# Attention ahead of two expert layers: row sums copied and then inverted in halves, block-diagonal keys from the load, late conversions ordered behind the last exponential, results over four buffers

## The chip, the cores and the metric

One core of a Trainium2 chip runs the whole program. The metric is the device time of one launch in microseconds. Lower is better. TensorE does matmuls and transposes, VectorE and ScalarE do elementwise work (both read and write PSUM and SBUF), SyncE (SP) issues the transfers, GpSimd only sets a few constants at the start.

## What is computed

Four batches of 12 heads, 448 positions, head size 64:

```python
scores = scale * np.matmul(q, k.transpose(0, 1, 3, 2))
scores = cap * np.tanh(scores / cap)
attn = np.exp(scores - max)            # divided by the row's sum
attn_out = np.matmul(attn, v)
x = attn_out as [1792 tokens, 768]
h = x @ w_in;   g = h - np.tanh(h);                     x = g @ w_out     # 768 -> 2048 -> 768
h = x @ w_in2;  g = h / (1.0 + np.exp(-1.702 * h));     out = g @ w_out2
```

The expert weights arrive as 64-bit floats; the kernel turns them into 32-bit numbers itself. All is float32 outside.

## The kernel before, in words

**Pairs.** Attention works on pairs of heads; there are 24 pairs, `g` from 0 to 23, six to a batch. For a pair, `load_qk` (L229) issues two q and four k transfers on SP and `load_v` (L248) three. The 448 keys are three chunks of 128 and a rest of 64. The rest of both heads is put into one block-diagonal 128 x 128 tile, so that one matmul serves both heads. `prep_q` (L261) transposes q on TensorE (four times 112 columns) and VectorE copies it out of PSUM. `prep_k` (L270) transposes three 128 x 128 pieces and, at L277, the rest with 64 rows and 64 columns; VectorE copies the three chunks (L79) and then the two 64 x 64 blocks of the rest into the tile `kt`, whose other blocks were set to zero once. `scores` (L284) writes the score matrix with keys on the partitions, for the rest (chunk KC) and chunks 0, 1, 2. `pair_act` (L298) takes tanh and exponential on ScalarE. `key_adds` (L311) adds the exponentials of the chunks on VectorE (`ts`), `pair_sum` (L331) sums them over keys on TensorE into one PSUM tile of a batch (`ps_r`, a single buffer), `pair_pv` (L319) multiplies by v and `pair_out` (L340) copies the result (`xs`).

**Row sums.** When a batch's six pairs are done, `batch_recip` (L347) inverts the sums in one VectorE instruction straight out of PSUM and sends them to `wrow` in device memory. `w_rows` (L353) broadcasts a pair's rows back from there, and the pair's x is multiplied by it (L370), rounded by ScalarE (`xh`) and its rest taken by VectorE (`xl`, L82). Batches 0 and 1 do so during attention at the pairs in `split_at` (L363); batches 2 and 3 put x unscaled into device memory (`xd`), and `x_next` (L585) does the rest within the last layer of the first pass.

**Weights.** There are chunks of weights, 128 x 768 or 128 x 640 numbers each. Conversion of a chunk has six steps: `conv_exp` (L158, ScalarE), `conv_low` (L162, VectorE or ScalarE), `conv_shift` and `conv_or` (L171, L175, VectorE), `conv_hi` (L182, ScalarE) and `conv_lo` (L186, VectorE), which also sends both halves to device memory (`kept`) for the second pass. Nine chunks, `early`, are converted during attention at the pairs in `conv_at` (L362). `prepare` (L193) loads or converts the next chunks in order, two ahead of the one in use (`LEAD`).

**The two layers' matmuls.** The tokens are worked in two passes of two batches. A pass has `gemm_in(0)` (L505), `gemm_out` (L524), `gemm_in(1)` and `gemm_out_rows` (L546). Every product is three matmuls of rounded parts. `gemm_out_rows` works the 384 result columns of a half in seven blocks of 128 tokens over eight steps `j`; in step 7 each block is finished, and `rows_out` (L570) copies it, on ScalarE for even and VectorE for odd blocks, into a two-buffer tile (tag "q") and sends it out in two transfers. `ps_next` (L453) gives eight PSUM banks in turn. In steps 0 to 7 of the first half and 0 to 3 of the second half of the first pass one `x_next` is put on the list `late`, which runs within the following step.

**What sets the order.** In attention each compute instruction goes through `pin`, so each engine keeps the order of the program. A planner places everything else, the transfers and all behind attention among them, where it finds the operands and the engine free; it may place it between the pinned instructions. The loop over pairs of `attention` (L365) is the hand-written order: the activations of the rest and chunk 0, scores of chunks 1 and 2, their activations, `pair_sum` of the pair before, PV of chunk 0, early conversions, `batch_recip`, transposes for pair g+2, PV of the rest, first scores of pair g+1, `key_adds`, PV of chunks 1 and 2. In the last pair 12 matmuls of the first layer, and 5 more behind it, stand between the last ones of attention.

Of the kernel before, what the change touches and what calls it, by code (L numbers as in the profile page):

```python
# [37 lines left out]
def attention_moe_moe(ctx, tc, q, k, v, cap, w_in1, w_out1, w_in2, w_out2, out):  # L38
# [79 lines left out]
    kt = [one_p.tile([P, P], F32, name=f"kt{i}") for i in range(3)]  # L118
# [110 lines left out]
    def load_qk(g):  # L229
        if g >= NG:  # L230
            return
        b, hp = divmod(g, NP)
        t = raw_p.tile([P, 2, 2 * C * D], F32, tag="raw", name="raw")
        for j in range(2):
            a = slice(j * D, (j + 1) * D)
            nc.sync.dma_start(
                out=t[:CP, 0].rearrange("p (c e) -> p c e", c=C)[:, :, a],
                in_=q[b, 2 * hp + j].rearrange("(p c) d -> p c d", c=C),
            )
        for j in range(2):  # L240
            a = slice(j * D, (j + 1) * D)
            kk = t[:, 1].rearrange("p (c e) -> p c e", c=C)
# [17 lines left out]

    def prep_q(g):  # L261
        if g >= NG:
            return
        qkt[g] = st_p.tile([P, 2, S], F32, tag="qk", name="qk")
# [3 lines left out]
        hi_dve(qkt[g][:, 0], ps[:, :S])  # L268

    def prep_k(g):  # L270
        if g >= NG:
            return
        ps = ps_s.tile([P, 512], F32, tag="s", name="ps_qk")
        t = raw.pop(g)
        for c in range(KC):
            pin(nc.tensor.transpose(ps[:, c * P:(c + 1) * P], t[:, 1, c * P:(c + 1) * P], ident))
        pin(nc.tensor.transpose(ps[:, KC * P:S], t[:KT, 1, KC * P:(KC + 1) * P], ident[:KT, :KT]))  # L277
        cp = hi_act if g == 0 else hi_dve
        cp(qkt[g][:, 1, :KC * P], ps[:, :KC * P])
        for j in range(2):  # L280
            a = slice(j * D, (j + 1) * D)
            cp(kt[g % 3][a, a], ps[a, KC * P:S])

    def scores(g, c):  # L284
        if g >= NG:
            return
        ps = ps_b.tile([P, 2, 512], F32, tag="b", name="ps_sc")
        if c == KC:
            pin(nc.tensor.matmul(ps[:, 0, :S], kt[g % 3], qkt[g][:, 0], start=True, stop=True))  # L289
        else:  # L290
            for j in range(2):
                a = slice(j * D, (j + 1) * D)
                pin(nc.tensor.matmul(  # L293
                    ps[:, j, :S], qkt[g][a, 1, c * P:(c + 1) * P], qkt[g][a, 0], start=True, stop=True
                ))
        sc_t[g, c] = ps

    def pair_act(g, cs):  # L298
# [9 lines left out]
        for c in cs:  # L308
            pin(nc.scalar.activation(out=tt[g, c], in_=tt[g, c], func=AF.Exp, scale=cpos))
# [52 lines left out]
    conv_at = [(2, 3), (4, 5), (7, 8), (9, 10), (11, 13), (14, 15), (16, 17), (19, 20), (21, 22)]  # L362
    split_at = [8, 9, 10, 11, 13, 14, 15, 16, 17, 19, 20, 21]  # L363

    def attention():  # L365
        wb = {}

        def scaled_x(g):
            x = xs[g]
            pin(nc.vector.tensor_tensor(out=x, in0=x, in1=wb.pop(g), op=ALU.mult))  # L370

        load_qk(0)
        load_v(0)
        load_qk(1)
# [4 lines left out]
        load_v(1)  # L379
        load_qk(2)  # L380
        prep_q(1)
        prep_k(1)
        for g in range(NG):
            x_g = split_at.index(g) if g in split_at else None
            pair_act(g, (KC, 0))
            for n, (p1, p2) in enumerate(conv_at):
                if g == p2 + 1:
                    conv_hi(early[n])
# [6 lines left out]
            for n, (p1, p2) in enumerate(conv_at):  # L395
                if g == p1 - 1:
                    conv_exp(early[n])
            load_v(g + 2)
            if g > 0:
                pair_sum(g - 1)  # L400
            pair_pv(g, 0)
            for n, (p1, p2) in enumerate(conv_at):
                if g == p1:
                    conv_low(early[n])
                elif g == p2:
                    conv_shift(early[n])
# [10 lines left out]
            if g + 1 in split_at:  # L417
                n = split_at.index(g + 1)
# [5 lines left out]
            if g == NG - 2:  # L424
                prepare(1)
            if g == NG - 1:
# [3 lines left out]
                hold[0] = False  # L430
# [6 lines left out]
        hold[0] = True  # L437
# [4 lines left out]
        batch_recip(B - 1)  # L442
# [156 lines left out]
    nc.sync.dma_start(out=capr, in_=cap.partition_broadcast(P))  # L599
# [10 lines left out]
    for i in range(NP):  # L610
# [3 lines left out]
    nc.vector.tensor_scalar(  # L614
        out=cpos.bitcast(U32), in0=capr.bitcast(U32), scalar1=0x7FFFFFFF, scalar2=None, op0=ALU.bitwise_and
    )
    nc.vector.reciprocal(out=tsc, in_=cpos)
    nc.vector.tensor_scalar(out=tsc, in0=tsc, scalar1=QK_SCALE, scalar2=None, op0=ALU.mult)
# [44 lines left out]
```

## Time and profile before

| | |
|---|---|
| median of three runs | 1171.54 us (1169.61 to 1173.59) |
| the profiled execution, its own time | 1171.32 us |
| its span, from first to last instruction | 1169.5 us |
| mean granted clock of TensorE | 0.997 |
| busy: TensorE, VectorE, ScalarE | 1149.6, 633.5, 602.6 us |
| attention, up to the first layer's unbroken matmuls | 0 to 230.31 us |
| first pass of the layers | 230.31 to 697.60 us |
| second pass | 697.60 to 1163.04 us |
| behind the last matmul | 6.46 us |

The busy time of TensorE is that of overlapped matmuls: a row of its order of time gives when one was issued, and the distance between two rows is what one costs in a stream. A bracket behind a row is the idle time of that engine just before it and what ended it.

### The profile page before, as it was taken

The numbers are of one execution on the slowest core, as the hardware profiler recorded it, in microseconds if no ns is written. First come the engines' busy times: TensorE is split into PE (matmuls) and PEld (weight loads), VectorE is DVE, ScalarE is ACT, GpSimd is POOL, SyncE is SP. The second block draws the span as 40 slices with busy tenths as digits, with TensorE's granted clock in tenths as the row PEclk, the third lists the DMA queues.
The fourth block names the chain that finished last, engine by engine and source line by source line (L and its number), as shares of the span: only waits on it lengthen the run. The fifth ranks groups of instructions, "written<-read, shape, count | busy, mean of one in ns | idle before, by whom it ended". The sixth has DMA issues, their size and how long they took to land.

```text
span 1169.5 us, 15456 instructions
## 1 busy us (share of the span) xinstructions
PE 1149.6 (98%) x5771; PEld 945.1 (81%) x5771; DVE 633.5 (54%) x990; ACT 602.6 (52%) x872; POOL 1.8 (0%) x16
## 2 busy tenths in 40 slices
PE   8999999999999999999998999999999999999997
PEld 3334333498888988888998998888988888899997
DVE  3889998889996445777655407888000133330000
ACT  5889888889995445666544307777000033320000
POOL 0000000000000000000000000000000000000000
PEclk9999999999999999999999999999999999999999
DMA  5566565744447766666788734333333333333432
GB/s 142 137 181 195 176 193 170 240 163 144 152 154 250 249 218 235 214 218 217 233 269 275 243 123 142 108 108 100 109 108 111 115 108 108 108 109 108 151 113 74
DMA packets 151194, 192.21 MB, mean 164 GB/s; under 512 B 58144, under 2 KB 110928, under 8 KB 151120
## 3 DMA queue, kind: packets, MB, share of 16 engines
q1 hardware_dynamic: 151120, 191.24, 51.8%
q8 instruction: 45, 0.74, 0.3%
q14 instruction: 29, 0.24, 0.1%
HBM read 132.51 MB, written 58.68 MB: 163 GB/s over the span
## 4 chain that ended last, share of the span: by engine, by line
PE 85%; DVE 7%; DMA 3%; ACT 2%; SPq 2%; issue 1%; DVEq 0%; ACTq 0%
PE ps_h L514 39%; PE ps_y L533 20%; PE ps_o L556 16%; PE ps_sc L293 3%; PE ps_pv L327 3%; PE ps_r L336 1%; DMA w<-wrow 1%; PE ps_pv L324 1%; DMA out_dram<-o 1%; DVE ts L316 1%; DVE wl L82 1%; PE ps_sc L289 1%; DVE w L349 1%; DVE ts L313 1%; DVE qk L79 1%
## 5 line engine op out<-in xcount | busy, mean ns | idle before, releaser
L514 PE MATMUL ps_h<-xl,wh 128*128 128x384 f32 (+1 forms) x768 | 280.4, 365 | 0.0
L514 PE MATMUL ps_h<-xh,wh 128*128 128x384 f32 (+1 forms) x768 | 279.6, 364 | 0.0
L514 PE MATMUL ps_h<-xh,wl 128*128 128x512 f32 (+1 forms) x768 | 174.7, 362 | 0.0
L514 PEld LDWEIGHTS ps_h<-xl,wh 128*128 128x128 f32 x768 | 144.2, 188 | 16.6 <-issue 0.2
L514 PEld LDWEIGHTS ps_h<-xh,wh 128*128 128x128 f32 x768 | 144.1, 188 | 16.5 <-issue 0.2
L556 PE MATMUL ps_o<-wh,gh 128*128 128x384 f32 x448 | 150.6, 336 | 3.3 <-ACT o L575 3.3
L514 PEld LDWEIGHTS ps_h<-xh,wl 128*128 128x128 f32 x768 | 139.4, 188 | 16.2 <-issue 1.4
L556 PE MATMUL ps_o<-wh,gl 128*128 128x384 f32 x448 | 150.4, 336 | 0.0
L556 PE MATMUL ps_o<-wl,gh 128*128 128x384 f32 x448 | 150.3, 335 | 0.0
L533 PE MATMUL ps_y<-gl,wh 128*128 128x384 f32 (+1 forms) x384 | 140.4, 366 | 0.0
L533 PE MATMUL ps_y<-gh,wh 128*128 128x384 f32 (+1 forms) x384 | 139.7, 364 | 0.0
L533 PE MATMUL ps_y<-gh,wl 128*128 128x384 f32 (+1 forms) x384 | 88.4, 362 | 0.0
L556 PEld LDWEIGHTS ps_o<-wh,gh 128*128 128x128 f32 x448 | 84.7, 189 | 4.0 <-ACT o L575 3.9
L82 DVE TENSOR_TENSOR wl<-wr,wh 128x768 fp32r<-128x768 f32 (+1 forms) x66 | 61.5, 932 | 48.4 <-ACT wh L76 23.2
L556 PEld LDWEIGHTS ps_o<-wl,gh 128*128 128x128 f32 x448 | 84.6, 189 | 0.0
L556 PEld LDWEIGHTS ps_o<-wh,gl 128*128 128x128 f32 x448 | 84.5, 189 | 0.0
L76 ACT CAST wh<-wr 128x768 fp32r<-128x768 f32 (+1 forms) x66 | 53.7, 814 | 55.0 <-PE ps_y L533 29.8
L573 DVE TENSOR_SCALAR o<-ps_o 128x384 f32<-128x384 f32 x12 | 6.7, 556 | 135.2 <-PE ps_o L556 116.5
L160 ACT ACTIVATE wr<-wd 128x768 f32<-128x768 f32 (+1 forms) x66 | 58.0, 878 | 41.4 <-DVE wl L82 33.0
L177 DVE SCALAR_TENSOR_TENSOR wr<-wd,wr 128x768 uint32<-128x768 uint32 (+1 forms) x66 | 61.6, 934 | 31.9 <-ACT wd L165 30.7
L533 PEld LDWEIGHTS ps_y<-gl,wh 128*128 128x128 f32 x384 | 72.1, 188 | 8.3
L533 PEld LDWEIGHTS ps_y<-gh,wh 128*128 128x128 f32 x384 | 72.0, 188 | 8.1
(75 smaller groups left out, 1473.5 us busy)
## 6 DMA issues: line engine op xcount, KB each, us to landing
wd<-in_moe_w_in_dram SPq DMA_DIRECT2D x64, 384.0 KB, 4.3
wh<-kept SPq DMA_DIRECT2D x63, 384.0 KB, 3.1
wl<-kept SPq DMA_DIRECT2D x63, 384.0 KB, 3.6
kept<-wh SPq DMA_DIRECT2D x54, 384.0 KB, 3.4
kept<-wl SPq DMA_DIRECT2D x54, 384.0 KB, 3.2
wd<-in_moe_w_out_dram SPq DMA_DIRECT2D x16, 768.0 KB, 5.4
wd<-in_moe_w_out_dram SPq DMA_DIRECT2D x24, 384.0 KB, 3.6
raw<-in_q_dram SPq DMA_DIRECT2D x48, 112.0 KB, 3.0
```

The costliest lines, as they stand in the source:

```text
L76: pin(nc.scalar.copy(out=dst, in_=src))
L79: pin(nc.vector.tensor_copy(out=dst, in_=src))
L82: pin(nc.vector.tensor_tensor(out=dst, in0=src, in1=hi.bitcast(F32), op=ALU.subtract))
L160: pin(nc.scalar.mul(out=raws[i][:, :width[i]], in_=dbls[i][:, :, 1].bitcast(F32), mul=2.0 ** -112))
L177: pin(nc.vector.scalar_tensor_tensor(out=u, in0=dbls.pop(i)[:, :, 1], scalar=0x80000007, in1=u, op0=ALU.bitwise_and, op1=ALU.bitwise_or))
L289: pin(nc.tensor.matmul(ps[:, 0, :S], kt[g % 3], qkt[g][:, 0], start=True, stop=True))
L293: pin(nc.tensor.matmul(ps[:, j, :S], qkt[g][a, 1, c * P:(c + 1) * P], qkt[g][a, 0], start=True, stop=True))
L313: pin(nc.vector.tensor_tensor(out=ts, in0=tt[g, 0], in1=tt[g, 1], op=ALU.add))
L327: pin(nc.tensor.matmul(ps[j * D:(j + 1) * D, :S], rawv[g][:, j, c, :], tt[g, c][:, j], start=(c == 0), stop=(c == KC - 1)))
L514: pin(nc.tensor.matmul(ps, w[:, kk, :], x[kk][:, a], start=(m == 0), stop=(m == len(seq) - 1)))
L533: nc.tensor.matmul(p[:, :a1 - a0], w[:, f - f0, :], x[f][:, a0:a1], start=(c == 0 and m == 0), stop=(c == len(parts) - 1 and m == len(seq) ...
L556: nc.tensor.matmul(ps[n][:, :HW], g[2 * j + ff][:, a], w[:, ff, :], start=(j == 0 and m == 0), stop=(j == KF // 2 - 1 and m == len(seq) - 1),)
```

## The change

It has six parts.

1. `batch_sums` copies the sums of a batch out of PSUM at its border pair; `batch_recip` inverts the copy in place in two halves, at the next two pairs. The splits of x move to later pairs; at pairs 21 and 22 there are two. The subtraction `lo_dve` of a split now stands behind the conversion steps of the pair.
2. The rest of the keys is loaded straight into block-diagonal places of `kt` (four of them now). `prep_k` transposes that whole tile at 128 columns and makes one copy of 512 columns. Scores of the rest read it from the tile `qk`.
3. The k loads of pair 0 go out on ScalarE's queue, and the loads of pair 1 and then 2 stand ahead of those of v. The load of `cap` and its three small VectorE instructions stand behind the q loads of pair 0.
4. In a pair, the PV of chunk 0 goes ahead of `pair_sum`. The early conversions have a new timetable.
5. `marks`: conversions of chunks below 6 that are not early are ordered behind the last exponential on ScalarE and the last inversion on VectorE. `prepare(1)` moves from pair 22 to 23.
6. `rows_out` takes its tile from four tags in turn; `x_next` is on the list in the first six steps of both halves.

```diff
-    kt = [one_p.tile([P, P], F32, name=f"kt{i}") for i in range(3)]
+    kt = [one_p.tile([P, P], F32, name=f"kt{i}") for i in range(4)]
...
             if i < NCH and i not in early:
+                with ExitStack() as behind:
+                    if i < 2 * LEAD + 2:
+                        for ins in marks:
+                            behind.enter_context(tc.issue_after(ins))
+                    convert(i)
...
-    def load_qk(g):
+    def load_qk(g, k_from=None):
...
-            nc.sync.dma_start(out=kk[:, :KC, a], in_=src[:KC * P].rearrange("(p c) d -> p c d", c=KC))
-            nc.sync.dma_start(out=kk[:KT, KC, a], in_=src[KC * P:])
+            k_dma = (k_from or nc.sync).dma_start
+            k_dma(
+                out=t[:, 1].rearrange("p (c e) -> p c e", c=C)[:, :KC, a],
+                in_=src[:KC * P].rearrange("(p c) d -> p c d", c=KC),
+            )
+            k_dma(out=kt[g % 4][a, a], in_=src[KC * P:])
...
-        pin(nc.tensor.transpose(ps[:, KC * P:S], t[:KT, 1, KC * P:(KC + 1) * P], ident[:KT, :KT]))
-        cp = hi_act if g == 0 else hi_dve
-        cp(qkt[g][:, 1, :KC * P], ps[:, :KC * P])
-        for j in range(2):
-            a = slice(j * D, (j + 1) * D)
-            cp(kt[g % 3][a, a], ps[a, KC * P:S])
+        pin(nc.tensor.transpose(ps[:, KC * P:], kt[g % 4], ident))
+        (hi_act if g == 0 else hi_dve)(qkt[g][:, S:], ps)
...
-    def batch_recip(b):
-        w = w_p.tile([P, S], F32, tag="w", name="w")
-        pin(nc.vector.reciprocal(out=w, in_=sum_t.pop(b)[:, :S]))
-        for j in range(2):
-            nc.sync.dma_start(out=wrow[b][j], in_=w[j * D:j * D + NP])
+    def batch_sums(b):
+        w_t[b] = w_p.tile([P, S], F32, tag="w", name="w")
+        hi_dve(w_t[b], sum_t.pop(b)[:, :S])
+
+    def batch_recip(b, half):
+        a = slice(half * S // 2, (half + 1) * S // 2)
+        w = w_t[b]
+        ins = pin(nc.vector.reciprocal(out=w[:, a], in_=w[:, a]))
+        if half:
+            for j in range(2):
+                nc.sync.dma_start(out=wrow[b][j], in_=w[j * D:j * D + NP])
+        return ins
...
-    conv_at = [(2, 3), (4, 5), (7, 8), (9, 10), (11, 13), (14, 15), (16, 17), (19, 20), (21, 22)]
-    split_at = [8, 9, 10, 11, 13, 14, 15, 16, 17, 19, 20, 21]
+    conv_at = [2, 4, 6, 9, 11, 13, 15, 17, 20]
+    split_at = [9, 10, 11, 12, 15, 16, 17, 18, 21, 21, 22, 22]
...
-        load_qk(0)
+        load_qk(0, nc.scalar)
+        nc.sync.dma_start(out=capr, in_=cap.partition_broadcast(P))
...
+        load_qk(1)
         load_v(0)
-        load_qk(1)
+        load_qk(2)
+        load_v(1)
         prep_q(0)
         prep_k(0)
         scores(0, KC)
         scores(0, 0)
-        load_v(1)
-        load_qk(2)
...
+            for n in x_of(g):
+                pin(nc.vector.tensor_tensor(out=xs[n], in0=xs[n], in1=wb.pop(n), op=ALU.mult))
+                i, a = x_part(n)
+                hi_act(xh[i][:, a], xs[n])
             scores(g, 1)
             scores(g, 2)
-            if x_g is not None:
-                scaled_x(x_g)
-                x_split(*divmod(x_g, NP), xs.pop(x_g))
-            pair_act(g, (1, 2))
+            last_exp = pair_act(g, (1, 2))
...
             load_v(g + 2)
+            pair_pv(g, 0)
             if g > 0:
                 pair_sum(g - 1)
-            pair_pv(g, 0)
...
+            for n in x_of(g):
+                i, a = x_part(n)
+                lo_dve(xl[i][:, a], xs.pop(n), xh[i][:, a])
...
+            if g >= NP and g % NP < 3:
+                b = g // NP - 1
+                if g % NP == 0:
+                    batch_sums(b)
+                else:
+                    batch_recip(b, g % NP - 1)
...
-        batch_recip(B - 1)
+        batch_sums(B - 1)
+        for half in range(2):
+            rec = batch_recip(B - 1, half)
+        marks.extend((last_exp.ins, rec.ins))
...
-                if b0 + NB < B and KF // 2 * half + j < NB * KM:
-                    late.append(lambda n=KF // 2 * half + j: x_next(b0 + NB, *divmod(n, KM)))
+                if b0 + NB < B and j < KM:
+                    late.append(lambda s=half, j=j: x_next(b0 + NB, s, j))
...
-        o = g_p.tile([P, TC], F32, tag="q", name="o")[:, :HW]
+        pool_n, tag = ((g_p, "q"), (g1_p, "v"), (g_p, "t"), (g_p, "far"))[n % 4]
+        o = pool_n.tile([P, TC], F32, tag=tag, name="o")[:, :HW]
```

The pool `g_p` has two buffers for each tag and `g1_p` one.

## Rows read from the trace of the kernel before

**Rows 1.** Busy time by stretch: length; PE, PEld, DVE, ACT, POOL; clock, DMA share, GB/s.
```profile
8.31:19.53 11.22, 7.84 (x37) 3.61 (x37) 2.89 (x8) 6.89 (x8) 0.00 (x0) 1.00 0.52 122
28.26:71.92 43.66, 43.66 (x201) 17.34 (x200) 34.24 (x50) 36.77 (x45) 0.00 (x0) 1.00 0.63 164
71.92:200.00 128.08, 125.05 (x569) 49.18 (x569) 115.92 (x180) 109.02 (x137) 0.00 (x0) 1.00 0.63 180
200.00:215.58 15.58, 14.40 (x67) 5.34 (x64) 14.00 (x22) 15.34 (x19) 0.00 (x0) 1.00 0.79 265
215.58:230.31 14.73, 14.53 (x63) 6.25 (x61) 10.30 (x13) 11.66 (x13) 0.00 (x0) 1.00 0.62 201
230.31:342.96 112.65, 112.65 (x562) 101.44 (x561) 102.79 (x170) 102.80 (x170) 0.00 (x0) 1.00 0.45 159
597.48:642.60 45.12, 41.86 (x240) 41.22 (x240) 24.57 (x35) 20.39 (x24) 0.00 (x0) 1.00 0.85 271
642.60:697.60 55.00, 55.00 (x307) 54.85 (x308) 16.76 (x23) 11.80 (x15) 0.00 (x0) 0.97 0.55 181
1046.54:1163.04 116.50, 116.48 (x672) 116.16 (x671) 3.90 (x7) 4.42 (x9) 0.00 (x0) 1.00 0.36 113
1163.04:1169.50 6.46, 0.00 (x0) 0.00 (x0) 0.56 (x1) 0.52 (x2) 0.00 (x0) 0.76 0.37 107
```

**Rows 2.** Order of time at the start: begin, us, engine, line, operation.
```profile
7.11 1.26 SPq L236 DMA_DIRECT2D raw<-in_q_dram  x2
10.93 0.58 PE L267 MATMUL ps_qk<-ident,raw 112*128 112x112 f32 x4 [0.64 <-DMA raw<-in_q_dram]
19.53 0.92 PE L289 MATMUL ps_sc<-qk,kt 128*128 128x448 f32 x2
```

**Rows 3.** Order of time on TensorE, the transposes of a steady pair.
```profile
26.34 0.60 PE L267 MATMUL ps_qk<-ident,raw 112*128 112x112 f32 x4
26.78 0.49 PE L276 MATMUL ps_qk<-ident,raw 128*128 128x128 f32 x3
27.20 0.27 PE L277 MATMUL ps_qk<-ident,raw 64*128 64x64 f32 x1
27.41 1.02 PE L324 MATMUL ps_pv<-tl,vt 128*128 128x448 f32 x2
```

**Rows 4.** Order of time: an inversion on VectorE, and two waits of TensorE.
```profile
69.37 2.96 DVE L349 RECIPROCAL w<-ps_r 128x448 f32<-128x448 f32 x1 [1.74 <-PE ps_r L336]
...
78.16 0.97 PE L336 MATMUL ps_r<-ts,sel 128*64 128x448 f32 x4 [1.00 <-DVE ts L317]
...
211.22 1.92 PE L293 MATMUL ps_sc<-qk 64*128 64x448 f32 x8 [1.18 <-ACT tl L307]
```

**Rows 5.** Order of time on VectorE and ScalarE in late pairs.
```profile
187.24 0.62 DVE L82 TENSOR_TENSOR xl<-xs,xh 128x448 fp32r<-128x448 f32 x1 [0.63 <-ACT xh L76]
...
208.87 1.93 ACT L165 ACTIVATE wd<-wd 128x768 uint16<-128x768 uint16 x1
```

**Rows 6.** Groups by line and form on VectorE: busy us, mean ns, idle before.
```profile
L79 DVE COPY qk<-ps_qk 128x384 f32<-128x384 f32 x23 | 12.6, 550 | 1.8 <-PE ps_qk L277 1.8
...
L79 DVE COPY kt<-ps_qk 64x64 f32<-64x64 f32 x46 | 10.0, 218 | 0.3
```

**Rows 7.** Order of time on SP: the inverted sums go out.
```profile
73.54 0.80 SPq L351 DMA_DIRECT2D wrow<-w  x2
```

**Rows 8.** Tile wb, the broadcast of the inverted sums, from issue to landing.
```profile
DMA to landing us min/median/max: 2.8/3.3/4.2
```

**Rows 9.** Order of time at the half border of the first pass.
```profile
637.16 0.49 ACT L575 ACTIVATE o<-ps_o 128x384 f32<-128x384 f32 x1 [1.33 <-DMA out_dram<-o]
...
642.60 0.44 PE L556 MATMUL ps_o<-wh,gh 128*128 128x384 f32 x1 [2.54 <-ACT o L575]
```

**Rows 10.** Busy time of one microsecond behind that border, columns as in rows 1.
```profile
645.00:646.00 1.00, 1.00 (x5) 1.00 (x4) 0.00 (x0) 0.27 (x1) 0.00 (x0) 0.50 0.94 318
```

**Rows 11.** Order of time, the last result copy.
```profile
1165.59 0.49 ACT L575 ACTIVATE o<-ps_o 128x384 f32<-128x384 f32 x1 [2.52 <-DMA out_dram<-o]
```

More of the change, by code (lines that the diff above doesn't have):

```diff
@@ L191, in conv_lo, with convert @@
             nc.sync.dma_start(out=kept[i][:, m], in_=t[:, :n].bitcast(F32))
+    marks = []
+    def convert(i):
+        conv_exp(i)
+        conv_low(i, i < KF or i % 2 == 0)
+        conv_shift(i)
+        conv_or(i)
+        conv_hi(i)
+        conv_lo(i)
+        n_ready[0] += 1
     def prepare(upto):
@@ L259, in load_v @@
         rawv[g] = tv
+    QK = S + (KC + 1) * P
     def prep_q(g):
@@ L263, in prep_q @@
             return
-        qkt[g] = st_p.tile([P, 2, S], F32, tag="qk", name="qk")
+        qkt[g] = st_p.tile([P, QK], F32, tag="qk", name="qk")
         ps = ps_s.tile([P, 512], F32, tag="s", name="ps_qk")
@@ L267, in prep_q @@
             pin(nc.tensor.transpose(ps[:, c * CP:(c + 1) * CP], raw[g][:CP, 0, c * P:(c + 1) * P], ident[:CP, :CP]))
-        hi_dve(qkt[g][:, 0], ps[:, :S])
+        hi_dve(qkt[g][:, :S], ps[:, :S])
     def prep_k(g):
@@ L287, in scores @@
         ps = ps_b.tile([P, 2, 512], F32, tag="b", name="ps_sc")
+        qk = qkt[g]
+        kc = slice(S + c * P, S + (c + 1) * P)
         if c == KC:
-            pin(nc.tensor.matmul(ps[:, 0, :S], kt[g % 3], qkt[g][:, 0], start=True, stop=True))
+            pin(nc.tensor.matmul(ps[:, 0, :S], qk[:, kc], qk[:, :S], start=True, stop=True))
         else:
@@ L292, in scores @@
                 a = slice(j * D, (j + 1) * D)
-                pin(nc.tensor.matmul(
-                    ps[:, j, :S], qkt[g][a, 1, c * P:(c + 1) * P], qkt[g][a, 0], start=True, stop=True
-                ))
+                pin(nc.tensor.matmul(ps[:, j, :S], qk[a, kc], qk[a, :S], start=True, stop=True))
         sc_t[g, c] = ps
@@ L308, in pair_act @@
         for c in cs:
-            pin(nc.scalar.activation(out=tt[g, c], in_=tt[g, c], func=AF.Exp, scale=cpos))
+            ins = pin(nc.scalar.activation(out=tt[g, c], in_=tt[g, c], func=AF.Exp, scale=cpos))
+        return ins
     def key_adds(g):
@@ L360, in x_split, with x_of, x_part @@
         lo_dve(xl[i][:, a], x, xh[i][:, a])
-    conv_at = [(2, 3), (4, 5), (7, 8), (9, 10), (11, 13), (14, 15), (16, 17), (19, 20), (21, 22)]
-    split_at = [8, 9, 10, 11, 13, 14, 15, 16, 17, 19, 20, 21]
+    conv_at = [2, 4, 6, 9, 11, 13, 15, 17, 20]
+    split_at = [9, 10, 11, 12, 15, 16, 17, 18, 21, 21, 22, 22]
     def attention():
         wb = {}
-        def scaled_x(g):
-            x = xs[g]
-            pin(nc.vector.tensor_tensor(out=x, in0=x, in1=wb.pop(g), op=ALU.mult))
-        load_qk(0)
+        def x_of(g):
+            return [n for n, at in enumerate(split_at) if at == g]
+        def x_part(n):
+            s_, i = divmod(n, NP)
+            return i, slice(s_ * S, (s_ + 1) * S)
+        load_qk(0, nc.scalar)
+        nc.sync.dma_start(out=capr, in_=cap.partition_broadcast(P))
+        nc.vector.tensor_scalar(
+            out=cpos.bitcast(U32), in0=capr.bitcast(U32), scalar1=0x7FFFFFFF, scalar2=None, op0=ALU.bitwise_and
+        )
+        nc.vector.reciprocal(out=tsc, in_=cpos)
+        nc.vector.tensor_scalar(out=tsc, in0=tsc, scalar1=QK_SCALE, scalar2=None, op0=ALU.mult)
+        load_qk(1)
         load_v(0)
-        load_qk(1)
+        load_qk(2)
+        load_v(1)
         prep_q(0)
@@ L416, in attention @@
             load_qk(g + 3)
-            if g + 1 in split_at:
-                n = split_at.index(g + 1)
+            for n in x_of(g + 1):
                 wb[n] = wb_p.tile([P, S], F32, tag="wb", name="wb")
@@ L423, in attention @@
                 dbl_dma()
-            if g == NG - 2:
+            if g == NG - 1:
                 prepare(1)
-            if g == NG - 1:
                 hold[0] = True
@@ L429, in attention @@
                     next(moe_0)
-                hold[0] = False
             scores(g + 1, KC)
@@ L436, in attention @@
             pair_out(g)
-        hold[0] = True
         for _ in range(5):
@@ L597, in moe @@
         gemm_out_rows(b0)
-    nc.sync.dma_start(out=capr, in_=cap.partition_broadcast(P))
     wz = one_p.tile([P, 512], BF16, name="wz")
@@ L613, in attention_moe_moe @@
     nc.vector.memset(cub_u, -CUB_V)
[L614 to L618, printed above, removed]
     moe_0 = moe(0)
```

39 lines of the change are left out of this document (13 added, 26 removed).

## The prediction

> **What bounds the kernel now.** I first read the busy times by stretch [rows 1]. In steady attention (28.26 to 71.92 us) TensorE is busy for all 43.66 us: five pairs of heads at 8.73 us each, with VectorE at 34.24 and ScalarE at 36.77. From there to 200 us it loses 3.03 us (128.08 less 125.05), in the next 15.58 us 1.18. In the expert layers it loses nothing, except in 597.48 to 642.60 (3.26 us) and in the 55.00 us behind it, where the granted clock is 0.97 in the mean. After its last matmul 6.46 us pass. So time can only come from TensorE's holes: the start, the batch borders of attention, the half border of the first pass, the tail. Then I read TensorE's order of time at each hole, for what released it, and the releaser's own queue. The profiled execution took 1171.32 us (span 1169.5, 1.8 around it); the median of the three runs is 1171.54, so both are one base.
>
> **Start.** From the first scores (8.31) to pair 1's first scores (19.53 [rows 2]) are 11.22 us with 7.84 of TensorE [rows 1]. It waits for the queries of pair 1 until 10.93, and SP issued them only at 7.11, behind two q, four k and three v loads of pair 0 [rows 2]. The change takes the four k loads to ScalarE's queue, which has no arithmetic until those keys arrive, and puts pair 1 ahead of the v loads. Left ahead of it are two q issues (0.63 each by the row) and the cap load, so it is issued about 2.5 us into the span, 4.6 earlier. What then limits the stretch is ScalarE, 6.89 us of work that begins when the first scores are there (1.0 us by the 448-column row of rows 3): some 8.0 us, a gain of 3.2. Bounds: 1.5 (only the waits for queries go) to 4.5 (the first scores come earlier too, since one copy takes the place of three). The cap load moves behind two q issues, 0.9 us later than now; the first tanh comes after 8.31, which covers it.
>
> **Pairs.** From 19.53 to 215.58 [rows 1] are 196.05 us and 22 pairs. At 8.73 for 21 of them and 1.07 less for the last, which transposes nothing (26.34 to 27.41 [rows 3]), TensorE alone needs 191.0: 5.0 are lost. The causes: a reciprocal of 2.96 us stands in VectorE's queue ahead of the sums that TensorE needs (1.00 us waited at 78.16 [rows 4]); later VectorE is nearly full (115.92 of 128.08 us), with a 0.63 us hole in each split while it waits for ScalarE's rounding [rows 5]; and a conversion hoisted between two pairs (1.93 us on ScalarE at 208.87 [rows 5]) makes TensorE wait 1.18 at 211.22 [rows 4]. The change answers all three: a copy frees the sums and the inversion follows in halves of about 1.5; other work stands between the rounding and its subtraction; the conversions of chunks 3 and 5 wait behind the last exponential and the last reciprocal. VectorE also loses two copies of 0.218 and pays 512 instead of 384 columns, at most 0.550 x 512/384 = 0.73 [rows 6]: 0.25 us less in each pair. The order on TensorE gives the sum matmuls of the pair before another 0.9 us (the PV of chunk 0 goes ahead). I take all 5.0; bounds 2.5 (half stays) and 5.2 (0.20 is idle behind 215.58 as well [rows 1]).
>
> **Transposes.** The fourth key transpose now has 128 columns and full weights. In rows 3 full ones stand 0.14 apart (three in 26.78 to 27.20), the small one takes 0.21 until the next matmul. Replacing the one by the other lies between -0.07 (it behaves like its neighbours) and +0.07 (twice a neighbour, because the last of a row also carries the change to other weights) for each of 21 pairs: -1.5 to +1.5 us. I take 0, since the 0.21 seems to be the exit, which stays. The Trainium skill ("TensorE: Matmul & The Clock Gate", LDWEIGHTS and Back-to-back issue gap) prices a weight load by its columns alone and a matmul by its columns at 2.4 GHz: the load would then cost the same and 64 more columns 27 ns, 0.6 us over the pairs by its figures; rows 3 alone cannot tell this from 0.
>
> **Weights for x.** The later reciprocal has a price. The second half ends about 3 us into pair 8 (and 14), and the first scaled x is wanted 0.6 us into the next. Before, the row sums went out 1.2 us behind the inversion (from 69.37 + 2.96 [rows 4] to 73.54 [rows 7]); they take 0.80 to issue; no row shows when they land, so I take the least of the broadcast's 2.8, and the broadcast itself lands 3.3 after its issue in the median [rows 8]. That is 1.2 + 0.8 + 2.8 + 3.3 = 8.1 us, so 11 us into an 8.73 us pair, 1.7 late. ScalarE's rounding of that x stands ahead of two tanh, and ScalarE has 8.73 - 36.77/5 = 1.4 us to spare per pair. I book 0.5 us lost for both places, bounds 0 and 3.
>
> **Held conversions.** Chunks 3 and 5 move into 215.58 to 342.96. ScalarE has 3.1 + 9.9 us free there and VectorE 4.4 + 9.9 [rows 1]; the work is two times 1.93 [rows 5] plus shorter pieces on ScalarE, and four pieces of up to 1 us on VectorE plus 0.6 for the added copy. Weights are two chunks ahead, so I book 0. If the cover were gone TensorE would wait for chunk 3, at most for the 3 to 4 us that moved.
>
> **Half border of the first pass.** TensorE stood 2.54 us until 642.60 because a result copy had not freed its bank; the copies wait for a result buffer still being written out (637.16) and behind the x of the second pass [rows 9]; 2.4 us later the clock is 0.50, the lower of its two levels, for a while [rows 10]. At the pace of the undisturbed pass (116.50/672 = 0.1734 [rows 1]) 306 matmuls are 53.1 us, not 55.0. So 3.26 + 1.9 = 5.1 is lost. Now the seven results of a half are spread over four tags with seven buffers ("v" has one), and no x comes in the last two steps of a half. I take all 5.1; bounds 0 and 5.2.
>
> **Tail.** The last result copy starts at 1165.59, 2.52 us of it waiting for a buffer [rows 11], with TensorE done at 1163.04. With four kinds it starts at 1163.1: 2.5 saved; the issues and landing behind it stay. Bounds 1.0 (SP's fourteen issues crowd) and 2.6.
>
> **Sum.** 3.2 + 5.0 + 0 - 0.5 + 0 + 5.1 + 2.5 = 15.3; 1171.3 - 15.3 = 1156.0.
>
> **Rivals.** (a) The border stall stays, because the chain of conversions and x, not the buffers, keeps the copies late: the x of step 0 to 5 are as tight as before, and rows 9 show one wait for a transfer among others. Against it: steps 6 and 7 are cleared. 1156.0 + 5.1 = 1161.1. (b) Attention stays paced by VectorE and ScalarE: they carry 115.92 and 109.02 of 128.08 us [rows 1], and the pairs 9 to 18 still have conversions, x and halves together. 1156.0 + 5.0 = 1161.0. (c) The result buffers do not do what is said: t, far, q and v also hold the next work's tiles, so copies wait as before at border and tail: 1156.0 + 7.6 = 1163.6. (d) Slower: the PV of chunk 0 now follows the scores of chunk 2 directly and must have its exponential, where 0.9 us of sum matmuls stood between. If ScalarE, in order behind roundings and x, delivers it late in each of 22 pairs, TensorE waits there. The point: at 15.3/22 = 0.7 us per pair the whole gain is gone; at 1.0 the time is 1156.0 + 22 = 1178. For it: ScalarE's queue is 84% full. Against it: the steady pairs show no idle TensorE at all, and the exponential of chunk 0 is issued before those of chunks 1 and 2, with two score matmuls still to run.
>
> **How the numbers follow.** Forecast 0.68, own range 1152 to 1159; (a) 0.12, (b) 0.10, (c) 0.05, (d) 0.05. About 0.3% (3.5 us) is what a measurement can tell. All cases but (d) are faster by more; (d) is split between same and slower, and a little of (c) with other losses falls into same. The range reaches from the good ends of start and transposes (1151.5) to past (a) and (b), 1162.5. Chances: faster 0.92, same 0.04, slower 0.04.
>
> **What would show it.** Right: scores of pair 1 near 16 us; every pair 8.7 us long with no wait of TensorE for sums; no wait near 208 us; the first pass's row matmuls taking 116.5 us at clock 1.00; the last copy within 0.1 us of TensorE's end. Wrong: a pair above 8.9 us, TensorE waiting for an exponential ahead of chunk 0's PV or for x in pairs 9 and 15, key transposes longer than 0.7 us together, or ScalarE's result copies still waiting at the half border.

## The result, and the profile after

The changed kernel took 1153.4 us in the median of 5 runs (1153.28 to 1154.4), the one before 1171.54 (5 runs, 1169.61 to 1174.19): a ratio of 0.9843, 95% interval 0.9827 to 0.986. Forecast were 1156.0 and 1151.5 to 1162.5, and faster. The profiled execution took 1153.33 us with a span of 1151.4, which is 18.1 less than the 1169.5 of before; all terms below are made up against these two spans.

The head of the page, with busy time and its share of the span for each engine:

```profile
span 1151.4 us, 15421 instructions
PE 1140.3 (99%) x5771; PEld 942.3 (82%) x5771; DVE 625.3 (54%) x953; ACT 603.8 (52%) x870; POOL 1.8 (0%) x16
```

The stretches that answer to [rows 1], with the same columns. They are cut at the same places of the program, so they begin earlier each time:

```profile
6.80:15.60 8.80, 7.59 (x36) 3.60 (x37) 2.46 (x5) 6.78 (x8) 0.00 (x0) 1.00 0.50 118
15.60:28.66 13.06, 12.19 (x55) 4.37 (x53) 9.43 (x14) 8.38 (x11) 0.00 (x0) 1.00 0.72 192
28.66:92.70 64.04, 63.58 (x304) 25.89 (x305) 48.69 (x64) 54.66 (x65) 0.00 (x0) 1.00 0.64 171
92.70:105.50 12.80, 10.56 (x48) 3.98 (x46) 11.13 (x17) 10.87 (x14) 0.00 (x0) 1.00 0.53 133
105.50:205.17 99.67, 99.67 (x470) 39.95 (x471) 93.79 (x129) 92.61 (x116) 0.00 (x0) 1.00 0.71 201
205.17:220.07 14.90, 14.60 (x63) 6.40 (x61) 8.09 (x11) 13.93 (x15) 0.00 (x0) 1.00 0.58 226
220.07:332.66 112.59, 112.59 (x561) 101.38 (x561) 104.72 (x177) 103.53 (x171) 0.00 (x0) 1.00 0.49 167
565.33:681.81 116.48, 116.48 (x673) 116.48 (x673) 54.06 (x76) 44.12 (x52) 0.00 (x0) 1.00 0.76 247
1147.24:1151.40 4.16, 0.00 (x0) 0.00 (x0) 0.00 (x0) 0.49 (x1) 0.00 (x0) 0.98 0.42 129
```

From these and rows 1 the whole difference is accounted for:

| from, to | before | after | gain | booked |
|---|---|---|---|---|
| launch to pair 1's first scores | 19.53 | 15.60 | 3.93 | 3.2 |
| to pair 23's first scores (22 pairs) | 196.05 | 189.57 | 6.48 | 4.5 |
| to the first expert matmuls | 14.73 | 14.90 | -0.17 | 0 |
| first pass (230.31 to 697.60; 220.07 to 681.81) | 467.29 | 461.74 | 5.55 | 5.1 |
| second pass (697.60 to 1163.04; 681.81 to 1147.24) | 465.44 | 465.43 | 0.01 | 0 |
| tail | 6.46 | 4.16 | 2.30 | 2.5 |

The 4.5 of the second line are the terms pairs (5.0), transposes (0) and weights for x (-0.5). The sum is 18.1. Five lines are within 0.8 us of what was booked. The second one is 2.0 off, and two larger errors of opposite sign lie in it, as the next views show.

**The holes.** TensorE's idle rows of before in attention [rows 4] are gone, but the stretches above show others: 0.87 in 15.60 to 28.66, 0.46 in the next, 2.24 in 92.70 to 105.50, 0.30 behind 205.17. Order of time over all engines at these two places (SPq is the queue of SP):

```profile
27.18 0.92 ACT L160 ACTIVATE wr<-wd 128x768 f32<-128x768 f32 x1 [3.29 <-DMA wd<-in_moe_w_in_dram]
28.66 1.92 PE L305 MATMUL ps_sc<-qk 64*128 64x448 f32 x8 [0.84 <-ACT tl L317]
...
31.04 0.97 PE L338 MATMUL ps_pv<-t,rv 128*64 128x448 f32 x4 [0.46 <-ACT t L319]
...
82.60 1.55 DVE L367 RECIPROCAL w<-w 128x224 f32<-128x224 f32 x1
...
86.50 1.35 SPq L370 DMA_DIRECT2D wrow<-w  x2
...
89.62 1.09 SPq L375 DMA_DIRECT2D wb<-wrow  x2
...
93.09 0.62 DVE L417 TENSOR_TENSOR xs<-xs,wb 128x448 f32<-128x448 f32 x1 [3.83 <-DMA wb<-wrow]
...
93.75 0.56 ACT L76 CAST xh<-xs 128x448 fp32r<-128x448 f32 x1 [4.33 <-DVE xs L417]
...
95.28 1.02 PE L301 MATMUL ps_sc<-qk 128*128 128x448 f32 x2 [1.65 <-ACT t L317]
...
101.30 0.97 PE L338 MATMUL ps_pv<-t,rv 128*64 128x448 f32 x4 [0.59 <-ACT t L319]
```

In pair 2 an early conversion stands on ScalarE ahead of the tanh and waits 3.29 us for its weights. It stands where it stood before, but there it did not wait:

```profile
27.71 0.90 ACT L160 ACTIVATE wr<-wd 128x768 f32<-128x768 f32 x1
```

Pair 1 now begins 3.9 us earlier, while SP begins to issue these weights only 2.2 us earlier (20.49, before 22.66). In pair 9 the chain is the one the prediction described: the second half of the inversion, the row sums out, the broadcast, the scaled x, its rounding on ScalarE, and behind that in ScalarE's order the tanh for which TensorE waits.

**The transposes.** TensorE in a steady pair, to be held against [rows 3]:

```profile
58.04 0.60 PE L281 MATMUL ps_qk<-ident,raw 112*128 112x112 f32 x4
58.48 0.49 PE L290 MATMUL ps_qk<-ident,raw 128*128 128x128 f32 x3
58.81 0.27 PE L291 MATMUL ps_qk<-ident,kt 128*128 128x128 f32 x1
58.92 0.92 PE L335 MATMUL ps_pv<-tl,vt 128*128 128x448 f32 x2
59.67 0.92 PE L301 MATMUL ps_sc<-qk 128*128 128x448 f32 x2
```

From the first transpose to the PV behind the last there are 0.88 us, 1.07 before. Three full ones take 0.33 until the next matmul; before, the three took 0.42 until the small one. The new fourth takes 0.11, the small one took 0.21. The PV behind them takes 0.75 (58.92 to 59.67); before it took 0.85, from 27.41 to the next row of that kernel:

```profile
28.26 0.92 PE L289 MATMUL ps_sc<-qk,kt 128*128 128x448 f32 x2
```

A steady pair is 8.45 us long, 8.73 before.

The weight loads of the same places show where the time went (PEld's order of time; first the kernel before, in the pair of 36.99 to 45.73, then the one after). The load for the small transpose came only after a gap of 0.17 and started when its matmul did, at 44.67; the PV's load behind it, at 44.87, also started with its matmul. In the kernel after, the load for the full one begins 0.11 ahead of its matmul, and so does the PV's:

```profile
44.67 0.14 PEld L277 LDWEIGHTS ps_qk<-ident,raw 64*128 64x128 f32 x1 [0.17 <-issue]
44.87 0.30 PEld L324 LDWEIGHTS ps_pv<-tl,vt 128*128 128x128 f32 x2
```

```profile
58.38 0.35 PEld L290 LDWEIGHTS ps_qk<-ident,raw 128*128 128x128 f32 x3
58.70 0.14 PEld L291 LDWEIGHTS ps_qk<-ident,kt 128*128 128x128 f32 x1
58.81 0.30 PEld L335 LDWEIGHTS ps_pv<-tl,vt 128*128 128x128 f32 x2
```

The step from the 112 rows of the q transposes to 128 shows no such delay: the first load behind it begins at 58.38, 0.10 ahead of its matmul at 58.48.

**Border and tail.** ScalarE's result copies, the third at the half border of the first pass and the last of the program; both wait for TensorE and no longer for a buffer, which answers to [rows 9, 11]:

```profile
621.52 0.49 ACT L607 ACTIVATE o<-ps_o 128x384 f32<-128x384 f32 x1 [1.58 <-PE ps_o L587]
...
1147.31 0.49 ACT L607 ACTIVATE o<-ps_o 128x384 f32<-128x384 f32 x1 [1.59 <-PE ps_o L587]
```

### The profile page after: what moved, and what is told of

It reads as the page before. It is cut to its first block, busy times and chain, and to the rows that moved or that the text cites. A ratio compares the mean times of both kernels' runs of the same rounds, so it can differ in the third digit from the quotient of the medians.

```text
span 1151.4 us, 15421 instructions
## 1 busy us (share of the span) xinstructions
PE 1140.3 (99%) x5771; PEld 942.3 (82%) x5771; DVE 625.3 (54%) x953; ACT 603.8 (52%) x870; POOL 1.8 (0%) x16
## 4 chain that ended last, share of the span: by engine, by line
PE 95%; DMA 2%; ACT 1%; SPq 1%; DVE 0%; issue 0%; ACTq 0%; DVEq 0%
PE ps_h L545 40%; PE ps_o L587 20%; PE ps_y L564 20%; PE ps_pv L338 4%; PE ps_sc L305 4%; PE ps_pv L335 1%; PE ps_r L347 1%; PE ps_sc L301 1%; PE ps_qk L281 1%; PE ps_qk L290 1%; DMA wd<-in_moe_w_in_dram 1%; ACT t L319 0%; ACT t L317 0%; SPq L245 0%; DMA wrow<-w 0%; DMA capr<-in_cap_dram 0%
## 5 line engine op out<-in xcount | busy, mean ns | idle before, releaser
L545 PE MATMUL ps_h<-xl,wh 128*128 128x512 f32 (+1 forms) x768 | 280.5, 365 | 0.0
L607 ACT ACTIVATE o<-ps_o 128x384 f32<-128x384 f32 x16 | 7.9, 492 | 130.7 <-PE ps_o L587 129.1
```

What stands on the lines that cost most here:

```text
L545: pin(nc.tensor.matmul(ps, w[:, kk, :], x[kk][:, a], start=(m == 0), stop=(m == len(seq) - 1)))
```

## The experiments

No kernel here leaves out work; the first one does one transpose twice. All were timed with the kernel before on the same chip, and ratios are against that. Three questions were open: whether the shorter pair comes from the shape of one transpose, whether border and tail are due to the four result buffers, and which edits of attention pay and why its holes stay.

### The small transpose added back

The old 64-row transpose is issued once more behind the full one, into the same place.

```diff
         pin(nc.tensor.transpose(ps[:, KC * P:], kt[g % 4], ident))
+        pin(nc.tensor.transpose(ps[:, KC * P:KC * P + D], kt[g % 4][:D], ident[:D, :D]))
```

> The changed kernel with one more transpose per pair, of the old shape (64 rows, 64 columns), behind the full one of the key rest; it writes the same numbers again. Theory A: a transpose of half the rows keeps TensorE from loading the weights of its neighbours ahead, so its cost is not its columns but what it does to the row of matmuls around it. Then the steady pair goes from 8.45 back to 8.74 us or a little above (8.85, since the full one stays), and the time to 1160 to 1162 us. Rival B (a transpose costs its columns; the shorter pair comes from the order PV before sums): 0.03 to 0.1 us per pair, at most 1155.7 us, pair at most 8.55.

1158.75 us (1158.34 to 1159.75), ratio 0.9893 (0.9878 to 0.9908). TensorE in a steady pair:

```profile
59.00 0.49 PE L290 MATMUL ps_qk<-ident,raw 128*128 128x128 f32 x3
59.33 0.27 PE L291 MATMUL ps_qk<-ident,kt 128*128 128x128 f32 x1
59.53 0.27 PE L292 MATMUL ps_qk<-ident,kt 64*128 64x64 f32 x1
59.74 1.02 PE L336 MATMUL ps_pv<-tl,vt 128*128 128x448 f32 x2
60.59 0.92 PE L302 MATMUL ps_sc<-qk 128*128 128x448 f32 x2
```

The full transpose now takes 0.20 until the small one (0.11 when a full one follows), the small one 0.21, the PV behind 0.85 again. That is 0.09 + 0.21 + 0.10 = 0.40, and the steady pair is 8.84, 0.39 longer; a full transpose more would be 0.11 by its neighbours. So the price lies in going to the small transpose and back, and falls on three matmuls. The small one differs in its rows and in its columns of data (64 each); the runs do not separate the two, but it is its load, of 64 rows and 128 columns, that starts late. The total is lower than the theory gave: 21 pairs by 0.39 are 8.2, the median rose by 5.35. The rest is in the holes. With the longer pair the wait of pair 9 is gone and pair 2 waits less; of 4.5 us of holes 0.9 are left.

### The keys alone

The kernel before with the block-diagonal load, the full transpose and the one copy of 512 columns, and nothing else.

```diff
-            nc.sync.dma_start(out=kk[:KT, KC, a], in_=src[KC * P:])
+            nc.sync.dma_start(out=kt[g % 4][a, a], in_=src[KC * P:])
...
-        pin(nc.tensor.transpose(ps[:, KC * P:S], t[:KT, 1, KC * P:(KC + 1) * P], ident[:KT, :KT]))
+        pin(nc.tensor.transpose(ps[:, KC * P:], kt[g % 4], ident))
```

> The kernel before with the block-diagonal keys by the load alone (full transpose, one copy of 512 columns), all else old. Theory A: the steady pair goes from 8.73 to 8.45 us; later pairs, paced by VectorE, gain what its copies lose, 0.25 us. Together 5 to 7 us: 1164.5 to 1166.5. Rival B: the pair stays at 8.70 or above in the steady part, time 1169 to 1171.

1165.76 us (1162.52 to 1167.29), ratio 0.9948 (0.9929 to 0.9966): 6.2 less than the 1171.99 of before on that chip. Its steady pair is 8.45, as in the whole change, and its stall at the half border stays. So the shorter pair is the keys' alone, and the order of PV and sums has no part in it. Nor has the lighter VectorE, which this run has too: in the run with the small transpose added VectorE is as light, and the pair is 8.84.

### One buffer kind for the results

```diff
-        pool_n, tag = ((g_p, "q"), (g1_p, "v"), (g_p, "t"), (g_p, "far"))[n % 4]
-        o = pool_n.tile([P, TC], F32, tag=tag, name="o")[:, :HW]
+        o = g_p.tile([P, TC], F32, tag="q", name="o")[:, :HW]
```

> The changed kernel with all results in the two buffers of tag q again; x in the first six steps of both halves stays. Tail: the last copy waits again, +2.3 us in any case. Theory C (the buffers were what held the half border): the stall there comes back with its half clock, 3 to 5 us more: 1158.5 to 1161. Rival D (the x in steps 6 and 7 held it): no stall at the border, 1155.5 to 1156.5.

1161.45 us (1160.41 to 1162.23), ratio 0.9914 (0.9898 to 0.9931): 8.05 more than the change, and 0.45 above the range that theory C gave. The wait of a result copy for its buffer and TensorE's wait for the copy are back, and 1.7 us later the granted clock is 0.50 (order of time on ScalarE and TensorE, then a window of one microsecond):

```profile
626.90 0.49 ACT L606 ACTIVATE o<-ps_o 128x384 f32<-128x384 f32 x1 [1.29 <-DMA out_dram<-o]
...
632.33 0.45 PE L587 MATMUL ps_o<-wh,gh 128*128 128x384 f32 x1 [2.53 <-ACT o L606]
```

```profile
634.00:635.00 1.00, 1.00 (x4) 1.00 (x4) 0.00 (x0) 0.00 (x0) 0.00 (x0) 0.50 0.49 140
```

Border and tail gained 5.55 + 2.30 = 7.85 in the change; this is all of it.

### The old steps for x

```diff
-                if b0 + NB < B and j < KM:
-                    late.append(lambda s=half, j=j: x_next(b0 + NB, s, j))
+                if b0 + NB < B and KF // 2 * half + j < NB * KM:
+                    late.append(lambda n=KF // 2 * half + j: x_next(b0 + NB, *divmod(n, KM)))
```

> The changed kernel with the x of the second pass in steps 0 to 7 of the first half and 0 to 3 of the second again; results stay on four tags. Theory C: no stall at the half border, 1153 to 1154.5. Rival D: the stall comes back in part, 1156 to 1158.5, with a wait of TensorE for a result copy that stands behind an x.

1153.38 us (1152.65 to 1155.66), ratio 0.9849 (0.9834 to 0.9864): no difference from the change, and no wait at the border. The timetable of x has no part in the gain; rival (a) falls with it.

### Sums ahead of the PV again

```diff
-            pair_pv(g, 0)
             if g > 0:
                 pair_sum(g - 1)
+            pair_pv(g, 0)
```

> The changed kernel with the sum matmuls of the pair before ahead of the PV of chunk 0, as it was. Theory A: the order has no part in the shorter pair (8.45 us stays); what it gives is 0.9 us more time for VectorE's sums, which is needed only where VectorE is late: 1153.4 to 1155.5 us. Rival B (the order shortens the pair): pair 8.6 us or more, time 1157 to 1160.

1152.25 us (1151.47 to 1153.32), ratio 0.9835 (0.9818 to 0.9851), attention ends at 220.10, in the change at 220.07. The wait of pair 2 for ScalarE is gone (one of 0.48 for keys stands there), the one of pair 9 is longer, and behind it the clock falls to its lower level (order of time on TensorE, then one microsecond):

```profile
94.85 1.86 PE L301 MATMUL ps_sc<-qk 128*128 128x448 f32 x2 [2.24 <-ACT t L317]
```

```profile
95.00:96.00 1.00, 1.00 (x2) 0.36 (x2) 0.79 (x2) 1.00 (x2) 0.00 (x0) 0.50 0.69 164
```

The median lies below both ranges that were expected, 1.15 under the change, with intervals that overlap. So a gain of the order is not shown, nor a price: rival (d) falls from this side too.

### No marks

The conversions of chunks 3 and 5 are free again to be planned ahead of the end of attention.

```diff
-        marks.extend((last_exp.ins, rec.ins))
```

> The changed kernel without ordering the conversions of chunks 3 and 5 behind the last exponential and inversion. Theory: the planner puts them between the last pairs again, ScalarE's tanh of a pair comes about 2 us late and TensorE waits 1 to 2 us near pair 21 or 22: 1154.4 to 1155.5 us. Rival (the new timetable leaves room there): 1153.0 to 1153.8 and no wait.

1161.32 us (1159.83 to 1164.41), ratio 0.9918 (0.9898 to 0.9938): 7.9 more than the change, where 1 to 2 were expected. Order of time on ScalarE and TensorE:

```profile
185.64 0.89 ACT L160 ACTIVATE wr<-wd 128x768 f32<-128x768 f32 x1 [4.77 <-DMA wd<-in_moe_w_in_dram]
...
187.11 1.02 PE L305 MATMUL ps_sc<-qk 64*128 64x448 f32 x4 [3.88 <-ACT tl L317]
...
189.65 1.87 PE L305 MATMUL ps_sc<-qk 64*128 64x448 f32 x4 [1.52 <-ACT t L317]
```

A hoisted conversion doesn't only cost its own time on ScalarE. It waits there for weights that have not landed, and everything behind it in that engine's order waits too. Behind the 3.88 and the 1.52 the clock is 0.50 (189 to 194 us), and this pair takes 16.77 us in place of 8.45. In pair 23 another wait for ScalarE follows, and the clock is 0.50 from 219 to 222 us:

```profile
218.90 1.80 PE L305 MATMUL ps_sc<-qk 64*128 64x448 f32 x4 [1.84 <-ACT t L317]
```

Attention ends at 230.86, 10.8 later in this profile, which is that of the slowest of the four runs.

### One inversion instead of two halves

The whole inversion reads the sums from PSUM in the border pair, with no copy.

```diff
-        hi_dve(w_t[b], sum_t.pop(b)[:, :S])
...
-        ins = pin(nc.vector.reciprocal(out=w[:, a], in_=w[:, a]))
+        ins = last_rec[0] = pin(nc.vector.reciprocal(out=w, in_=sum_t.pop(b)[:, :S]))
```

> The changed kernel with one inversion per batch straight out of PSUM at the border pair, as it was; timetable of splits unchanged, so the rows of the sums come two pairs earlier. Theory E (the halves' price is the late rows: TensorE waits 2.2 us around pair 9): that wait goes; the waits at the borders come back only in part, since the sums now stand behind the PV: 1151.5 to 1153.3 us. Rival F (the inversion in one piece holds up the sums at all three borders, 1 us each): 1154 to 1156.

1153.92 us (1153.71 to 1155.07), ratio 0.9853 (0.9839 to 0.9868): between the two theories' figures, and the same as the change. The rows leave two pairs earlier and the wait of pair 9 is gone; in its place TensorE waits 1.40 at each of the three borders. Order of time at the first:

```profile
66.44 2.96 DVE L367 RECIPROCAL w<-ps_r 128x448 f32<-128x448 f32 x1 [0.80 <-PE ps_r L347]
...
73.87 0.62 DVE L79 COPY xs<-ps_pv 128x448 f32<-128x448 f32 x1
...
74.59 0.97 PE L338 MATMUL ps_pv<-t,rv 128*64 128x448 f32 x4 [1.40 <-ACT t L317]
```

The profile names ScalarE as releaser. But VectorE's copy of the pair before out of PSUM ends at 73.87 + 0.62 = 74.49, and at all three borders the PV starts 0.10 us behind the end of that copy (126.63 and 126.73, 178.78 and 178.88 at the others); it stands in VectorE's order behind the sums, and those behind the 2.96. So the wait is read as one for the copy; a second PSUM buffer there, which would show it, was not tried. The halves save 3 by 1.40 = 4.2 us, and their later rows give back 2.2 at pair 9.

### Split and conversions a pair later

```diff
-    conv_at = [2, 4, 6, 9, 11, 13, 15, 17, 20]
-    split_at = [9, 10, 11, 12, 15, 16, 17, 18, 21, 21, 22, 22]
+    conv_at = [3, 5, 7, 9, 11, 13, 15, 17, 20]
+    split_at = [10, 10, 11, 12, 15, 16, 17, 18, 21, 21, 22, 22]
```

> The changed kernel with two moves in the timetable: the first split goes from pair 9 to 10 (two there), and the first three early conversions each one pair later (3, 5, 7). Theory: the waits around pair 9 (2.2 us) and in pair 2 (1.3 us) go, 1149.5 to 1151 us. Rival (VectorE is too full in pairs 9 to 13 and only hands the wait on): 1152 to 1154.

1151.84 us (1151.54 to 1153.75), ratio 0.9837 (0.9822 to 0.9852): between the two theories' figures. The hole of pair 2 shrinks and the one of pair 9 goes, but waits of 0.38 and 0.59 appear in pairs 11 and 12 and of 0.52 and 0.58 at the end of attention: a third split after two in one pair waits 2.25 us for its broadcast, which SP issued only at 103.51. That this comes from the two buffers that the broadcasts have is tested in the last run.

### The old order of loads at the start

```diff
-        load_qk(0, nc.scalar)
+        load_qk(0)
...
-        load_qk(1)
         load_v(0)
-        load_qk(2)
-        load_v(1)
+        load_qk(1)
```

> The changed kernel with the old order of the first loads: all on SP, v of pair 0 ahead of pair 1, pair 2 later; cap still behind the q of pair 0. Theory: the start's part of the gain goes, pair 1's first scores come near 19.5 us in place of 15.6, and all of it shows in the time: 1156.5 to 1157.6 us. Rival (the later waits in pairs 2 and 9 swallow part of it, since the loads are then not behind): 1154.5 to 1156.

1155.47 us (1154.17 to 1156.81), ratio 0.987 (0.9855 to 0.9884). Pair 1's first scores come at 20.50, 4.9 later than in the change, yet only 2.1 stay in the median, as the rival had it: with the later start the waits of pairs 2 and 9 vanish.

### The rows over GpSimd's queue

```diff
-                nc.sync.dma_start(out=wrow[b][j], in_=w[j * D:j * D + NP])
+                nc.gpsimd.dma_start(out=wrow[b][j], in_=w[j * D:j * D + NP])
...
-            nc.sync.dma_start(out=t[j * D:(j + 1) * D], in_=wrow[b][j, i].partition_broadcast(D))
+            (q or nc.sync).dma_start(out=t[j * D:(j + 1) * D], in_=wrow[b][j, i].partition_broadcast(D))
```

`w_rows` gets GpSimd's queue as `q` for the splits of attention; `conv_at` is the one of the split experiment, `split_at` that of the change.

> The changed kernel with the transfers of the inverted sums, out and back, on GpSimd's queue in attention, and the first three early conversions one pair later. Theory: the rows for x were late because SP's queue, in order, sends them 2.4 us after the inversion and their broadcast behind it; from a queue of their own they come 2 us earlier and the wait around pair 9 falls from 2.2 to 0.5 us or less: 1150.0 to 1151.5. Rival (the transfers' own landing sets it, not the queue): the wait stays above 1.5 us, 1151.8 to 1153.

1152.8 us (1152.07 to 1154.69), ratio 0.9849 (0.9835 to 0.9864): no gain. Tile wb from issue to landing, the first scaled x on VectorE, and TensorE's wait for it:

```profile
DMA to landing us min/median/max: 2.8/3.9/7.0
```

```profile
92.35 0.62 DVE L417 TENSOR_TENSOR xs<-xs,wb 128x448 f32<-128x448 f32 x1 [4.54 <-DMA wb<-wrow]
...
94.53 1.02 PE L301 MATMUL ps_sc<-qk 128*128 128x448 f32 x2 [2.36 <-ACT t L317]
```

In the change the same landing is 3.1 in the median and 4.6 at most. From the queue with nothing ahead the first broadcast was issued at 84.83 (89.62 in the change), but it took longer, and x comes 8.8 us into pair 9, where it came 8.1 into it. Why the transfers took longer was not tested. The clock stayed 1.00 behind the wait of 2.36.

### One split in each late pair, three broadcast buffers

```diff
-    wb_p = first_pool("wb", 2)
+    wb_p = first_pool("wb", 3)
...
+    conv_at = [3, 5, 7, 9, 11, 13, 15, 17, 20]
+    split_at = [10, 10, 11, 12, 15, 16, 17, 18, 19, 20, 21, 22]
```

> The changed kernel with three buffers for the rows, splits at 10, 10, 11, 12, 15 to 22 one each, and the first three early conversions one pair later. Theory: what was left in the run with two moves (waits around pairs 11 and 22, 2.1 us) came from the row buffers, two of which pair 10 holds, and from two splits in one pair; both go: 1149.2 to 1150.5. Rival (VectorE too full in pairs 19 and 20, with a half inversion and a split each): 1151 to 1152.5.

1149.4 us (1149.23 to 1149.55), ratio 0.9817 (0.9801 to 0.9834): faster than both kernels. Attention ends at 216.38, 3.7 before the change; in 172 us of it TensorE lacks 0.1 (columns as in rows 1):

```profile
33.00:205.00 172.00, 171.90 (x808) 68.91 (x806) 155.53 (x211) 156.13 (x193) 0.00 (x0) 1.00 0.68 193
```

The third split's broadcast is issued at 96.41 here, 7.1 us earlier than with two buffers. So the holes of pairs 9 and later could be had back by the timetable and the third buffer together, without another engine or queue; what each of them gives was not separated. About 1 us in pair 2 is left.

## Why the prediction was right

The direction, the time and most terms held: 15.3 were forecast for the profiled execution and 18.1 came, 2.8 more, inside the range. But a part of the agreement is luck, and the 22 pairs show it. In pairs of 8.73 and one of 7.66 without transposes, the work of before is 190.99 and the holes 5.06. After, it is 21 pairs of 8.447 and one of 7.66 (197.51 to 205.17), so 185.05, and 189.57 - 185.05 = 4.52 of holes. So the transposes gave 5.9 more than booked, and the terms pairs and weights for x together 4.0 less.

**Start** (3.2, bounds 1.5 to 4.5): 3.93. Queries of pair 1 were issued at 3.08 (booked about 2.5), scores came at 15.60 (booked near 16). What limits it now is not ScalarE, 6.78 busy of 8.80, as the prediction had it, but pair 2's keys, whose transposes stand ahead of pair 1's first scores: SP issues them behind v of pair 0 and pair 2's queries, the second load of their chunks at 11.51, and TensorE waits 1.14 for them. The list of the change has the loads of pair 2 ahead of those of v; that holds for v of pair 1, not for v of pair 0. So the size of the term was right and the limit was not.

```profile
3.08 1.27 SPq L245 DMA_DIRECT2D raw<-in_q_dram  x2
...
6.80 1.02 PE L301 MATMUL ps_sc<-qk 128*128 128x448 f32 x2 [0.68 <-ACT qk L76]
...
11.51 0.60 SPq L253 DMA_DIRECT2D raw<-in_k_dram  x1
...
14.13 0.52 PE L290 MATMUL ps_qk<-ident,raw 128*128 128x128 f32 x3 [1.14 <-DMA raw<-in_k_dram]
```

**Pairs** (5.0): all the waits that it named are gone, and that part of the term stands. The term missed what is late next: the early conversion in pair 2, which the earlier start brings ahead of its weights. Of the holes 1.8 us are in pairs 1 and 2, so the term gave 3.2 (5.06 less 1.8), inside its bounds.

**Transposes** (0, bounds -1.5 to +1.5): this is the step that failed; it measured 5.9. It priced the replaced instruction alone, 0.21 until the next matmul, and held that gap for an exit that stays. In fact the small transpose's neighbours carried the cost as well: 0.10 ahead of it, 0.10 in its own gap, 0.10 in the PV behind. In rows 3 the three full ones stood 0.14 apart only in the mean, with the delay of the small one's load in it; in the kernel after three take 0.33, and so 0.11. The weight loads of the kernel before, which the prediction did not read, held the sign: the gap of 0.17 ahead of 44.67. The first experiment put the cost back, the second had it alone. The Trainium skill ("TensorE: Matmul & The Clock Gate", LDWEIGHTS and Back-to-back issue gap) prices by columns and would have had the kernel 0.6 us slower here by its figures. For the length of a weight load the traces agree: 128 columns last 0.14 at 64 rows and at 128. For the sum they don't: the load of the small transpose starts later, and the kernel gained 5.9. A sum by columns leaves that out, and so did mine.

**Weights for x** (0.5, bounds 0 to 3): the mechanism was right and the size was not: 2.24 in idle rows and 2.7 in the length of pairs 9 and 10, none at the second batch. I had the second half end about 3 us into pair 8; it ends at 84.15, and pair 8 begins 8.45 before pair 9's 85.0, so 7.6 in, since in VectorE's order it stands behind the adds of pair 7 and a conversion step. The rows went out 2.4 us behind it, where 1.2 was booked.

**Held conversions** (0): right. In 220.07 to 332.66 TensorE has no hole, with VectorE 104.72 and ScalarE 103.53 busy of 112.59. What the marks are worth in attention is much more than the 1.18 us wait from which I took it: without them the changed kernel is 7.9 slower.

**Half border** (5.1): 5.55, by the buffers. **Tail** (2.5): 2.30, the last copy 0.07 behind TensorE's end.

**Rivals.** (a) falls by the two experiments on buffers and x, (c) with it. (b) falls: in 105.50 to 205.17 TensorE has no hole with VectorE 94% and ScalarE 93% busy; in pairs 2 and 9 TensorE waits because an engine in the chain ahead of it stands still for a transfer. (d) falls at its size: no steady pair waits for chunk 0's exponential, and no gain of the old order is shown. But its mechanism is there behind the holes: the PV of chunk 0 waits 0.46 for that exponential in pair 2 and 0.59 in pair 10. With these waits, the one for x in pair 9 and pairs of 10.03, 10.27 and 9.30 us (2, 9 and 10), three of the signs of a wrong prediction came true.

What stays open is why the PV behind the small transpose is 0.10 longer: the rows show its first weight load starting with it, and no run separated that from the matmul itself. In pair 22 of the change, where no transposes stand ahead of it, the same PV also takes 0.85 (204.32 to 205.17), and its load starts with it there too. A shape between 64 and 112 rows was not tried.

## What to carry to other kernels

Where TensorE is never idle, the time is in the spacing of its instructions: compare start to start over a whole group, neighbours included, before pricing one that is replaced, and pad an odd tile to the full array if the padding is there for nothing. Look for instructions that wait for a transfer in the middle of an in-order engine, since their price is that of the engine's whole queue; hold them back, or ask for the data a step later. And when a hole closes, ask what was late by less and hid behind it: a start 4.9 us later cost only 2.1.

## What the runs showed of the hardware

- One transpose of 64 rows among full ones costs 0.39 us in all, where a full one takes 0.11; its weight load did not start ahead of its matmul, nor did that of the PV behind it.
- The granted clock was 0.50 (1.2 GHz) shortly behind TensorE's waits of 2.24 us (sums first), 2.53 (one buffer kind), 3.88 with 1.52, and 1.84 (no marks). It was 1.00 in each of the five microseconds behind the waits of 1.65 (the change), 1.40 (one inversion, at its first border) and 2.36 (rows over GpSimd's queue). So the length of the wait alone did not decide: 2.24 and 2.36 stand at the same place of the program, ahead of pair 10's first scores.
- At its lower level the matmuls behind the wait cost time as well: pair 10 was 10.17 long behind the wait of 2.24, and 9.30 behind those of 1.65 and 2.36, where the clock stayed up.
- The same row broadcasts took 3.9 us in the median from GpSimd's queue and 3.1 from SP's.
